# Windowed attention with a token-mixing layer on one core: a kernel planned in Python in place of one written batch by batch

## The chip, the core and the metric

The kernel runs on one core of a Trainium2 chip. Its time is the device time of one execution in microseconds; the median of several runs counts. The engines are TensorE (PE; its weight loads are PEld), VectorE (DVE), ScalarE (ACT), GpSimd (POOL) and SyncE (SP). Each takes its own instructions in the order in which they stand in the program and waits for semaphores of the others. Products of TensorE are written to PSUM, eight banks of 512 f32 per partition, from where VectorE and ScalarE copy them to SBUF.

## What is computed

Eight batches of 576 positions, 8 heads of 64. First attention with a window of 128 positions and a linear distance penalty, then a layer that mixes positions, on the attention's output x (576 x 512 per batch).

```python
# attention, per batch and head
scores = q @ k.T / 8 - 2.0**-(h+1) * |i - j|      # only where 0 <= i - j < 128
x[:, 64*h : 64*h+64] = softmax(scores) @ v
# mixing, per batch
mixed = ((x @ w_q) @ (x @ w_k).T / 8) @ x
out = relu(mixed) @ w_out
```

Inputs and output are f32 in DRAM; the kernel computes in f16 with f32 sums.

## The kernel before

**Tiling.** Positions go in tiles of 128, 128, 128, 128 and 64. The scores are kept transposed, keys on the partitions: for key tile kb the queries 128 kb to 128 kb + 255 are the only ones that the window lets through, so a head has five products of 256, 256, 256, 192 and 64 queries, 1024 columns in all, two PSUM banks.

**Loads** (`c_load`, L98 to L119). All on GpSimd's queue, with a cast from f32 to f16: per batch ten of q and k and five of v, each 128 (or 64) positions by 8 heads by 64. The tiles of q and k have one buffer each, so the loads of the next batch wait until TensorE has transposed this batch's.

**Attention.** `mk_xpose` (L121) transposes q and k, four heads' pairs at a time, and copies them out of PSUM. `mk_qk2` (L135) makes the scores of two heads into two PSUM tiles; ScalarE takes exp of 1024 columns (L152), VectorE multiplies by the table of exp(-slope * distance), zero outside the window (L153). `mk_pv` (L157) multiplies with V for one query tile and four heads (L179); V has a column of ones, so that the row sums come with it. VectorE divides (L182, L183). `mk_xt` (L189) transposes x.

**Mixing** (`moe_chunks`, L216). `wq` and `wk` project; the sum is regrouped as (x w_q) ((x w_k)^T x), so `gmat` (L248) makes a 64 x 512 matrix per batch; `mk_mixed` (L258) multiplies and takes relu; `mk_out` (L272) projects, copies to f32 and stores on SyncE's queue.

**Order.** Written by hand: the steps of attention of batch b stand in twelve chunks, and after each chunk one of mixing of batch b - 1. A framework moves instructions a little by their dependencies and gives each engine its list. All eight batches pass in this way, and the mixing of the last one stands alone at the end.

## Time and profile before

| | |
|---|---|
| time, median of 3 runs | 246.55 us (246.26 to 247.41) |
| span of the profiled execution | 246.7 us |
| TensorE busy | 211.7 us (86%), 1864 products |
| VectorE busy | 142.0 us (58%), 362 instructions |
| ScalarE busy | 121.5 us (49%), 218 instructions |
| GpSimd busy | 106.6 us (43%), 132 instructions |
| DMA from GpSimd's queue | 114096 packets, 14.82 MB |

Matmuls are pipelined, and a product's shown duration holds its way through the array; what a product costs in a row of them is the distance between the starts of two. The clock column is the one that the throttle granted to TensorE: 1.00 is 2.4 GHz, 0.50 is 1.2 GHz. At the start of the execution the column is 1.00 without a record of the clock, and there the distances of the starts have to be read instead.

### The profile page before, as it was taken

Reading aid. Unit: us, or ns where it says so; the run is one execution under the profiler, and the core shown is the slowest. Engines: PE = TensorE matmul, PEld = TensorE weight load, DVE = VectorE, ACT = ScalarE, POOL = GpSimd, SP = SyncE. Lnnn points to the kernel's source line nnn. Section 1 sums busy time; section 2 is a strip of 40 time slices with the busy share of each in tenths; the row PEclk is TensorE's granted clock in tenths of the full one; section 3 lists DMA queues with packets and bytes.
Section 4 is the critical chain, followed back from the end, with each engine's and each line's share of the span. In section 5 each row is a group of like instructions: output and inputs, shape, how many; then the busy total and the mean of one; then the engine's idle time right before and its main releaser. Section 6 shows DMA issues by size and latency. Waiting matters only on the chain.

```text
span 246.7 us, 4766 instructions
## 1 busy us (share of the span) xinstructions
PE 211.7 (86%) x1864; PEld 128.1 (52%) x1864; DVE 142.0 (58%) x362; ACT 121.5 (49%) x218; POOL 106.6 (43%) x132
## 2 busy tenths in 40 slices
PE   0367799889997999889997999889988999889783
PEld 0134576455564656456554656446554656556331
DVE  1124763567645775577556674667656774577413
ACT  2986505880179305970289106950389007930240
POOL 9999938900694019800792039700891000000000
PEclk9999999957996599857995599858995699759979
DMA  3999999972699039962999139922999131003204
GB/s 24 104 141 148 155 112 113 131 50 73 123 166 121 14 117 159 155 39 85 133 163 104 43 90 179 154 20 108 129 161 84 47 125 26 0 0 130 64 24 168
DMA packets 119366, 24.55 MB, mean 100 GB/s; under 512 B 114224, under 2 KB 114736, under 8 KB 119344
## 3 DMA queue, kind: packets, MB, share of 16 engines
q0 software_dynamic: 114096, 14.82, 93.3%
q1 hardware_dynamic: 5248, 9.44, 10.8%
q8 instruction: 14, 0.23, 0.4%
q14 instruction: 8, 0.07, 0.1%
HBM read 29.62 MB, written 9.44 MB: 158 GB/s over the span
## 4 chain that ended last, share of the span: by engine, by line
PE 65%; ACT 13%; DVE 7%; POOL 6%; issue 6%; DMA 2%; ACTq 0%; POOLq 0%
PE po L279 19%; PE px L179 15%; PE ptr L130 7%; PE pxt L198 5%; PE pw L226 4%; PE pk L240 3%; ACT rm L268 2%; DVE osb L51 2%; PE pm L266 2%; DMA vnat<-in_v_dram 2%; ACT qT L49 1%; POOL vnat L113 1%; ACT gm L49 1%; DVE invr L182 1%; PE pg L252 1%
## 5 line engine op out<-in xcount | busy, mean ns | idle before, releaser
L113 POOL DMA_DIRECT2D vnat<-in_v_dram x40 | 34.4, 885 | 77.5 <-issue 59.3
L49 ACT COPY qT<-ptr 128x512 f16<-128x512 f16 (+1 forms) x24 | 12.4, 517 | 80.8 <-PE ptr L130 80.8
L279 PE MATMUL po<-wout_sb,rm 128*128 128x512 f16 x160 | 50.4, 451 | 0.7 <-ACT rm L268 0.2
L143 PEld LDWEIGHTS <-kT 64*128 64x128 f16 x320 | 27.4, 106 | 25.5 <-issue 17.7
L51 DVE COPY osb<-po 128x512 f32<-128x512 f32 (+1 forms) x40 | 27.6, 690 | 19.6 <-PE po L279 19.2
L279 PEld LDWEIGHTS <-rm 128*128 128x128 f16 x160 | 17.1, 116 | 17.3 <-issue 10.1
L182 DVE RECIPROCAL invr<-px 128x4 f32<-128x4 f32 (+1 forms) x80 | 13.3, 175 | 19.8 <-PE px L179 18.3
L51 DVE COPY kT<-ptr 128x512 f16<-128x512 f16 (+1 forms) x24 | 9.1, 381 | 20.0 <-PE ptr L130 18.8
L268 ACT ACTIVATE rm<-pm 128x512 f16<-128x512 f32 x32 | 19.7, 631 | 0.5 <-PE pml L267 0.5
L266 PE MATMUL pm<-wqT,gm 64*128 64x512 f16 x32 | 14.1, 474 | 5.8 <-ACT gm L49 0.7
L51 DVE COPY xT<-pxt 128x512 f16<-128x512 f16 (+1 forms) x40 | 15.5, 388 | 1.0 <-PE pxt L198 0.5
L49 ACT CAST wqT<-pw 64x512 f16<-64x512 f32 x8 | 4.6, 579 | 16.8 <-PE pwl L228 16.8
L49 ACT COPY kT<-ptr 128x512 f16<-128x512 f16 x16 | 9.4, 586 | 5.8 <-PE ptr L130 5.8
L226 PE MATMUL pw<-xT,wqk_sb 128*64 128x512 f16 x32 | 10.1, 416 | 0.0
L51 DVE COPY qT<-ptr 128x512 f16<-128x512 f16 x16 | 6.7, 421 | 3.0 <-PE ptr L130 2.3
L269 ACT ACTIVATE rm<-pml 128x64 f16<-128x64 f32 x32 | 8.5, 264 | 0.0
L51 DVE CAST wkn<-pk 128x256 f16<-128x256 f32 (+1 forms) x16 | 4.4, 315 | 5.6 <-PE pk L240 5.6
L252 PEld LDWEIGHTS <-wkn 128*64 128x64 f16 (+1 forms) x40 | 3.7, 108 | 7.4 <-issue 3.3
L266 PEld LDWEIGHTS <-gm 64*128 64x128 f16 x32 | 3.0, 95 | 8.0 <-ACT gm L49 1.0
L240 PE MATMUL pk<-wqk_sb,xT 128*128 128x64 f16 (+1 forms) x160 | 7.1, 195 | 0.0
L267 PE MATMUL pml<-wqT,gm 64*128 64x64 f16 x32 | 6.7, 208 | 0.0
L240 PEld LDWEIGHTS <-xT 128*128 128x128 f16 (+1 forms) x160 | 5.8, 100 | 1.5 <-issue 0.2
(752 smaller groups left out, 562.0 us busy)
## 6 DMA issues: line engine op xcount, KB each, us to landing
out_dram<-osb SPq DMA_DIRECT2D x32, 256.0 KB, 2.0
vnat<-in_v_dram POOLq DMA_DIRECT2D x32, 128.0 KB, 5.0
out_dram<-osb SPq DMA_DIRECT2D x8, 128.0 KB, 4.0
vnat<-in_v_dram POOLq DMA_DIRECT2D x8, 64.0 KB, 4.7
wout_sb<-in_moe_w_out_dram POOLq DMA_DIRECT2D x1, 512.0 KB, 6.2
qnat_107<-in_q_dram POOLq DMA_DIRECT2D x1, 128.0 KB, 3.5
knat_109<-in_k_dram POOLq DMA_DIRECT2D x1, 128.0 KB, 3.4
qnat_111<-in_q_dram POOLq DMA_DIRECT2D x1, 128.0 KB, 3.4
```

What stands on the lines that cost most here:

```text
L49: eng.copy(out_ap, in_ap)
L51: eng.tensor_copy(out=out_ap, in_=in_ap)
L113: nc.gpsimd.dma_start(out=vnat[:n, kt, 0:H, 1:65], in_=v[b, :, ss, :].transpose([1, 0, 2]))
L130: nc.tensor.transpose(pt[:, c, :n], src, identh[:n, :n])
L143: nc.tensor.matmul(pss[i][:, o : o + w], kT[hb : hb + 64, hp, 128 * kb : 128 * kb + 128], qT[hb : hb + 64, hp, 128 * kb : 128 * kb + w], s ...
L179: nc.tensor.matmul(px[:, hh, :], lt, rt, start=(i == 0), stop=(i == len(mms) - 1))
L182: nc.vector.reciprocal(out=invr[:n], in_=px[:n, :, 0])
L226: nc.tensor.matmul(pw[0:64], wqk_sb[:, dc, 0:64], xT[:, dc, 0:512], start=(dc == 0), stop=(dc == 3))
L240: nc.tensor.matmul(pk[:n, t, :], xT[:, dc, 128 * t : 128 * t + n], wqk_sb[:, dc, 64:128], start=(dc == 0), stop=(dc == 3))
L266: nc.tensor.matmul(pm, lt, st_["wqT"][:, 0:512], start=True, stop=True)
L268: nc.scalar.activation(out=rm[:, db, 0:512], in_=pm, func=AF.Relu, scale=WSCALE)
L279: nc.tensor.matmul(po, rm[:, db, lo : lo + 128], wout_sb[:, db, :], start=(db == 0), stop=(db == 3))
```

## The change

The kernel is written anew. A small planner in Python (`Plan`) is given about 600 steps, each with the engines that may run it, an assumed duration for each, a priority, what it reads and writes, and how many PSUM banks it needs. It lays the steps out in assumed time, picks an engine for the copies that ScalarE or VectorE can make, assigns the banks (four double slots), and the program is emitted in that order; the framework keeps it.

- **Loads.** q, k and v of two batches come in one DMA of 128 x 16 x 64 (the first two batches' q and k in separate ones), into double buffers. The last 64 positions of two batches share one tile of 128. v of the first two batches, and the weights, come as f32 over SyncE's queue and are cast by ScalarE and VectorE.
- **Transposes.** Eight of 128 columns into one bank, copied out as 1024 columns at once.
- **Scores.** A unit is two heads and half of the key tiles: two banks, six or four products, in turn for the one head and the other, whose operands lie on partitions 0 to 63 and 64 to 127. One exp and one multiply of 1024 columns each as before, eight per batch.
- **Products with V.** 18 for two heads, over all five query tiles, always with 128 keys: the rows beyond the last key are zero in V, and the probabilities are padded. One reciprocal and one division for 2 x 5 x 64 columns, four of each a batch.
- **x transposed** two heads at a time, one copy of 576 columns.
- **Mixing.** The query projection is made twice over (128 columns of weights), in two halves of 288 queries; the Gram step in two halves of 256 columns that land on partitions 0 to 63 and 64 to 127; the mixed products in pairs on the two halves of the rows. The output of the last 64 positions is made for two batches in one tile, so there are 36 output tiles in place of 40.
- **Set-up.** The distance table is made of iota and VectorE's comparisons, 512 columns a head, and copied for the second form.

```diff
-        chunks = [[c_load, mk_xpose(0, 0), mk_xpose(1, 0), mk_xpose(0, 1), mk_xpose(1, 1)],
...
-    for b in range(NB):
-        ac, ast = attn_chunks(b)
...
+class Plan:
+    LAT = 0.10
...
+                    st = max(free.get(e, 0.0), t, tp)
+                    cand.append((st, o, e, dur))
+            assert cand, "the plan is stuck"
+            st0 = min(c[0] for c in cand)
+            near = [c for c in cand if c[0] <= st0 + 0.06]
+            st, o, e, dur = min(near, key=lambda c: (c[1].prio, c[1].seq, c[0] + c[3]))
+            for g in o.ps_new:
+                _, _, s, h = place(g, held)
+                g.slot = (s, h)
+                held[g.cls] = held.get(g.cls, 0) + g.banks
+                for i in range(g.banks):
+                    halves[s][h + i] = g
+            o.start, o.eng = st, e
+            free[e] = st + dur
...
+
+def act_t(n):
+    return 0.14 + 0.000833 * n
+
+
+def dve32_t(n):
+    return 0.13 + 0.00104 * n
+
+
+def dve16_t(n):
+    return 0.13 + 0.00052 * n
+
+
+PERIOD = 14.8
+NPT = 6
...
+    plan = Plan(4, {"score": 4, "other": 6})
...
+    def load(name, dst, src, n, prio, writes, merged=False):
+        plan.op(name, {"POOL": 0.47 + 0.00047 * n}, lambda e: nc.gpsimd.dma_start(out=dst, in_=src),
+                prio, writes=writes, lat=-0.00095 * n)
...
+                else:
+                    load("ldqk", nat[x][p % 2][:, j].rearrange("t b (h d) -> t (b h) d", h=H),
+                         src[2 * p : 2 * p + 2, :, tk, :].rearrange("b h t d -> t (b h) d"), 2048, t0,
+                         [("nat", x, p % 2, j, b) for b in range(2)])
...
+                    n = TN[t]
+                    load_f32("ldvf", osb[t][:n].rearrange("t (h d) -> t h d", h=H),
+                             v[b, :, 128 * t : 128 * t + n, :].transpose([1, 0, 2]), 8 * n, 64,
+                             t0 + 30 * b, [("osb", t)])
+                for t in range(NT):
+                    n = TN[t]
+                    cast("cv", vn[0][:n, t, b, :, 0:D], osb[t][:n].rearrange("t (h d) -> t h d", h=H), 512,
+                         -10 + 20 * b, [("osb", t)], [("vn", 0, t, b)])
...
+        for h in range(H):
+            def table(e, h=h):
+                nc.scalar.activation(out=bt[:, 1, h], in_=wm, func=AF.Exp, scale=-(2.0 ** (-(h + 1))))
+            plan.op("table", {"ACT": 0.6}, table, t0, reads=["wm"], writes=[("bt1", h)])
...
+                def tr(e, c=c, x=x, g=g):
+                    for hp in range(4):
+                        for j in range(2):
+                            o = hp * 256 + j * 128
+                            nc.tensor.transpose(ps16(g)[:, o : o + 128],
+                                                nat[x][pb][:, 2 * c + j, i, 128 * hp : 128 * hp + 128], idn)
+
+                def ev(e, c=c, x=x, g=g):
+                    cp(e, qkT[pb][:, i, x, :, 256 * c : 256 * c + 256],
+                       ps16(g).rearrange("t (a n) -> t a n", a=4))
+
+                plan.op("tqk", {"PE": 0.46}, tr, t0, ps_new=[g],
+                        reads=["idn"] + [("nat", x, pb, 2 * c + j, i) for j in range(2)])
+                plan.op("etqk", both(1024, True), ev, t0, ps_read=[g], writes=[("qkT", pb, i, x, c)])
...
+    CHUNK = [[(0, 0, 256), (1, 256, 256)], [(2, 0, 256), (3, 256, 192), (4, 448, 64)]]
...
+                def sc(e, hp=hp, c=c, g=g):
+                    for kb, o, w in CHUNK[c]:
+                        for a in range(2):
+                            r = slice(64 * a, 64 * a + 64)
+                            nc.tensor.matmul(ps32(g)[:, 512 * a + o : 512 * a + o + w],
+                                             qkT[pb][r, i, 1, hp, 128 * kb : 128 * kb + 128],
+                                             qkT[pb][r, i, 0, hp, 128 * kb : 128 * kb + w],
+                                             start=True, stop=True)
+
+                def ex(e, c=c, pt=pt, g=g):
+                    nc.scalar.activation(out=pt[:, c, 0:1024], in_=ps32(g), func=AF.Exp, scale=SCALE)
+
+                def mu(e, hp=hp, c=c, pt=pt):
+                    o = pt[:, c, 0:1024]
+                    nc.vector.tensor_tensor(
+                        out=o, in0=o, in1=bt[:, c, 2 * hp : 2 * hp + 2].rearrange("t h c -> t (h c)"),
+                        op=ALU.mult)
+
+                rd = [("qkT", pb, i, x, cc) for x in range(2) for cc in ((0, 1) if c == 0 else (1, 2))]
+                plan.op("sc", {"PE": 0.27}, sc, t0 + c * 1.5, ps_new=[g], reads=rd + ["pads"])
+                plan.op("exp", {"ACT": 0.95}, ex, t0 + c * 1.5, ps_read=[g], writes=[("pt", n, c)])
+                plan.op("mul", {"DVE": 0.68}, mu, t0 + c * 1.5,
+                        reads=["bt%d" % c and ("bt0", hp)], writes=[("pt", n, c)])
...
+            def pv(e, hp=hp, pt=pt, g=g):
+                for a in range(2):
+                    h = 2 * hp + a
+                    for t in range(NT):
+                        mm = []
+                        for kb, off in ((t - 1, 128), (t, 0)):
+                            if kb < 0:
+                                continue
+                            c = 0 if kb < 2 else 1
+                            o = 512 * a + (448 if kb == 4 else 256 * (kb % 2)) + off
+                            mm.append((pt[:, c, o : o + 128], vn[pb][:, kb, i, h, :]))
+                        for x, (lt, rt) in enumerate(mm):
+                            o = 512 * a + (D + 1) * t
+                            nc.tensor.matmul(ps32(g)[:, o : o + D + 1], lt, rt,
+                                             start=(x == 0), stop=(x == len(mm) - 1))
...
+            def nrm(e, hp=hp, iv=iv, g=g):
+                px = ps32(g).rearrange("t (a c) -> t a c", a=2)[:, :, 0 : NT * (D + 1)]
+                px = px.rearrange("t a (j e) -> t a j e", j=NT)
+                nc.vector.reciprocal(out=inv[iv], in_=px[:, :, :, D])
+                nc.vector.tensor_tensor(
+                    out=xs[i][:, :, 128 * hp : 128 * hp + 128].rearrange("t j (a d) -> t a j d", a=2),
+                    in0=px[:, :, :, 0:D],
+                    in1=inv[iv].unsqueeze(3).broadcast_to([P, 2, NT, D]),
+                    op=ALU.mult)
+
+            plan.op("pv", {"PE": 0.60}, pv, t1, ps_new=[g],
+                    reads=[("pt", n, 0), ("pt", n, 1)] + [("vn", pb, t, i) for t in range(NT)])
+            plan.op("nrm", {"DVE": 1.02}, nrm, t1, ps_read=[g], writes=[("xs", i, hp)])
...
+            def xt(e, hp=hp, g=g):
+                for t in range(NT):
+                    m = TN[t]
+                    nc.tensor.transpose(ps16(g)[:, lo[t] : lo[t] + m],
+                                        xs[i][:m, t, 128 * hp : 128 * hp + 128], idn[:m, :m])
+
+            def ext(e, hp=hp, g=g):
+                cp(e, xT[i][:, hp, 0:S], ps16(g)[:, 0:S])
+
+            plan.op("xt", {"PE": 0.30}, xt, t2, ps_new=[g], reads=[("xs", i, hp)])
+            plan.op("ext", both(S, True), ext, t2, ps_read=[g], writes=[("xT", i, hp)])
...
+        def mwq(e):
+            for c in range(2):
+                for dc in range(4):
+                    nc.tensor.matmul(ps32(g2)[:, 512 * c : 512 * c + 288], wqq[:, dc, :],
+                                     xT[i][:, dc, 288 * c : 288 * c + 288], start=(dc == 0), stop=(dc == 3))
...
+        def mg(e):
+            for t in range(NT):
+                m = TN[t]
+                for a in range(2):
+                    nc.tensor.matmul(ps32(g3)[64 * a : 64 * a + 64, 0:256], wkn[i][:m, t, :],
+                                     xs[i][:m, t, 256 * a : 256 * a + 256], start=(t == 0), stop=(t == NT - 1))
...
+                def mm(e, c=c, j=j, g=g4):
+                    for a in range(2):
+                        r = slice(64 * a, 64 * a + 64)
+                        nc.tensor.matmul(ps32(g)[:, 512 * a : 512 * a + 288], gm[i][r, 128 * j : 128 * j + 128],
+                                         wqT[i][r, 288 * c : 288 * c + 288], start=True, stop=True)
...
+            def mo(e, o=o, g=g5):
+                for db in range(4):
+                    nc.tensor.matmul(ps32(g), rm[pb][:, db, o : o + 128], wout[:, db, :],
+                                     start=(db == 0), stop=(db == 3))
+
+            def eo(e, n=n, g=g5):
+                cp(e, osb[n], ps32(g))
...
+            to = t0 + 6 + z * PERIOD / len(tiles)
+            rd = [("rm", pb, y, c, j) for y in ((i,) if t < 4 else (0, 1)) for c in range(2) for j in range(2)]
+            plan.op("po", {"PE": 0.90}, mo, to, ps_new=[g5], reads=rd + [("wout", c) for c in range(4)])
+            plan.op("eo", both(512), eo, to, ps_read=[g5], writes=[("osb", n)])
+            plan.op("st", {"SP": 0.2}, st, to, reads=[("osb", n)], lat=2.0)
...
+    order = plan.run()
+    with tc.manual_schedule():
+        for o in order:
+            o.emit(o.eng)
```

Where the order moved, at three places. ScalarE's list from the last exp of a batch to the first of the next, in the middle of the program. Before (`rm` is the relu of the mixing of the batch before, `qT` and `kT` the copies of the next batch's transposes, `ptr` their PSUM tile, `pw` that of the query projection):

```order
L152 ACTIVATE pt_1057<-ps_1_1043 128x1024
L268 ACTIVATE rm<-pm 128x512
L269 ACTIVATE rm<-pml 128x64
L54 ACTIVATE vnat<-identh 128x45
L54 ACTIVATE kT<-bfull_88 128x4x64
L49 COPY qT<-ptr 128x4x128
L49 COPY kT<-ptr 128x4x128
L49 CAST wqT<-pw 64x512
L49 CAST wqT<-pwl 64x64
...
L152 ACTIVATE pt_1399<-ps_0_1387 128x1024
```

After, from the last exps of the seventh batch into those of the eighth (`pt`; `psl` is any PSUM slot, `xT` the transposed x, `osb` an output tile of an earlier batch, `wkn`, `wqT` projections):

```order
L436 ACTIVATE pt_84<-psl_110 128x1024
L436 ACTIVATE pt_84<-psl_111 128x1024
L240 COPY xT_93<-psl_109 128x576
L240 COPY osb_106<-psl_110 128x512
L436 ACTIVATE pt_85<-psl_111 128x1024
L436 ACTIVATE pt_85<-psl_109 128x1024
L240 COPY xT_93<-psl_110 128x576
L436 ACTIVATE pt_86<-psl_111 128x1024
L240 COPY osb_103<-psl_110 128x512
L436 ACTIVATE pt_86<-psl_109 128x1024
L240 COPY osb_104<-psl_110 128x512
```

Before, the copies of a batch stand together between two blocks of exps; in the middle of the new list one to four exps stand side by side, and copies of this batch and of others stand between them.

ScalarE's list at the start, up to the first exp. Before (`bfull` are the tables, `wm` the distances):

```order
L64 ACT_TABLE_LOAD
L64 CAST identh<-ident_68 128x128
L49 COPY qT<-ptr 128x4x128
L84 ACTIVATE bfull_88<-wm 128x1024
...
L54 ACTIVATE kT<-bfull_88 128x4x64
L49 COPY kT<-ptr 128x4x128
L49 COPY qT<-ptr 128x4x128
...
L152 ACTIVATE pt_209<-ps_0_197 128x1024
```

After (`vn` is V, `osb` an output tile that holds V in f32 for the time being, `bt` the tables, `wkf` and `rm` hold weights in f32):

```order
L240 ACT_TABLE_LOAD
L240 CAST vn_77<-osb_107 64x8x64
L240 CAST vn_77<-osb_103 128x8x64
L240 CAST vn_77<-osb_104 128x8x64
L331 ACTIVATE bt<-wm 128x512 x8
L240 CAST wkw<-wkf 128x256
L240 COPY qkT_79<-psl_109 128x4x256
L240 CAST wout<-rm_102 128x512 x2
L436 ACTIVATE pt_81<-psl_110 128x1024
```

Three casts of V, which wait for loads on SyncE's queue, now stand ahead of the tables, and three casts of weights ahead of the first exp.

TensorE's list in the attention of a batch. Before (`po` is an output tile of the batch before, `px` the product with V of one query tile, `pt` the probabilities of one head, `x` the result that is transposed into `pxt`):

```order
L279 LDWEIGHTS rm
L279 MATMUL po<-wout_sb,rm 128x512
...
L179 LDWEIGHTS pt_1819
L179 MATMUL px<-vnat,pt_1819 128x65
...
L179 LDWEIGHTS pt_1822
L179 MATMUL px<-vnat,pt_1822 128x65
...
L198 LDWEIGHTS x_1929
L198 MATMUL pxt<-identh,x_1929 128x128
```

After (the rows of one pair of heads, of the next pair's scores, of an output tile and of the scores again):

```order
L465 LDWEIGHTS pt_84
L465 MATMUL psl_108<-vn_78,pt_84 128x65
L430 LDWEIGHTS qkT_80
L430 MATMUL psl_111<-qkT_80 128x256
...
L582 LDWEIGHTS rm_101
L582 MATMUL psl_110<-wout,rm_101 128x512
...
L430 LDWEIGHTS qkT_80
L430 MATMUL psl_109<-qkT_80 128x192
```

Before, products with V run over eight heads for one query tile, and the transposes of x follow tile by tile; now 18 products of one pair of heads stand together, and scores, output products and transposes of three batches alternate.

## Rows read from the trace of the kernel before

**Rows 1.** Windows: busy of PE, PEld, DVE, ACT, POOL; clock; DMA share; GB/s.

```profile
117.00:146.00 29.00, 26.98 (x248) 16.63 (x248) 18.29 (x49) 13.94 (x26) 12.58 (x16) 0.82 1.10 112
```

**Rows 2.** Longest wait: engine, line, releaser: us in total, times, longest.

```profile
ACT qT L49 <- PE ptr L130: 80.8, 8, 11.5
```

**Rows 3.** Chain of work that ended last: start us, us, engine, tile, line.

```profile
126.90 0.59 ACT pt_1822 L152
154.22 0.59 ACT pt_2242 L152
...
229.75 0.55 PE pw L226 x2
236.64 6.06 PE po L279 x20
```

**Rows 4.** Timeline of TensorE early: start us, us, engine, line, operation.

```profile
30.72 0.62 PE L198 MATMUL pxt<-identh,x_286 128*128 128x128 f16 x4
31.13 0.32 PE L179 MATMUL px<-vnat,pt_209 128*128 128x65 f16 x2
...
43.47 0.28 PE L143 MATMUL ps_1_548<-qT,kT 64*128 64x256 f16 x1
43.47 0.28 PE L143 MATMUL ps_0_547<-qT,kT 64*128 64x256 f16 x1
```

**Rows 5.** Timeline of TensorE, 59 to 64 us, at the higher clock.

```profile
59.46 0.22 PE L179 MATMUL px<-vnat,pt_559 128*128 128x65 f16 x2
...
59.95 0.39 PE L198 MATMUL pxt<-identh,x_709 128*128 128x128 f16 x4
60.41 1.02 PE L279 MATMUL po<-wout_sb,rm 128*128 128x512 f16 x4
61.27 0.33 PE L179 MATMUL px<-vnat,pt_559 128*128 128x65 f16 x2
...
63.41 0.40 PE L198 MATMUL pxt<-identh,x_748 128*128 128x128 f16 x4
```

**Rows 6.** Half a microsecond in which the clock falls (columns as above).

```profile
48.50:49.00 0.50, 0.50 (x6) 0.27 (x3) 0.44 (x1) 0.50 (x3) 0.50 (x2) 0.70 2.30 147
```

**Rows 7.** Timeline of ScalarE in the attention of a batch.

```profile
49.58 1.04 ACT L152 ACTIVATE pt_613<-ps_1_599 128x1024 f16<-128x1024 f32 x1
50.48 0.62 ACT L268 ACTIVATE rm<-pm 128x512 f16<-128x512 f32 x1
```

**Rows 8.** Groups by form: count | busy us, mean ns | idle before.

```profile
L49 ACT COPY kT<-ptr 128x512 f16<-128x512 f16 x16 | 9.4, 586 | 5.8 <-PE ptr L130 5.8
L51 DVE COPY osb<-po 128x512 f32<-128x512 f32 x32 | 22.1, 689 | 17.3 <-PE po L279 16.9
L51 DVE COPY kT<-ptr 128x512 f16<-128x512 f16 x16 | 6.8, 425 | 17.6 <-PE ptr L130 17.5
```

**Rows 9.** Timeline of VectorE in the attention of a batch.

```profile
52.06 0.18 DVE L182 RECIPROCAL invr<-px 128x4 f32<-128x4 f32 x1 [0.70 <-PE px L179]
52.27 0.42 DVE L183 TENSOR_TENSOR x_646<-px,invr 128x256 f16<-128x256 f32 x1
52.62 0.68 DVE L153 TENSOR_TENSOR pt_634<-pt_634,bfull_100 128x1024 f16<-128x1024 f16 x1
53.21 0.68 DVE L153 TENSOR_TENSOR pt_637<-pt_637,bfull_102 128x1024 f16<-128x1024 f16 x1
```

**Rows 10.** Timeline of the start: first load, first exp.

```profile
2.17 1.08 POOL L104 DMA_DIRECT2D qnat_107<-in_q_dram  x1
...
17.23 1.02 ACT L152 ACTIVATE pt_209<-ps_0_197 128x1024 f16<-128x1024 f32 x1 [0.70 <-PE ps_0_197 L143]
```

**Rows 11.** Timeline of GpSimd's loads of q and k for the second batch.

```profile
24.31 1.06 POOL L104 DMA_DIRECT2D qnat_432<-in_q_dram  x1
25.17 1.07 POOL L107 DMA_DIRECT2D knat_434<-in_k_dram  x1
```

**Rows 12.** DMA issues: tile, queue, count, KB, median us from issue to landing.

```profile
vnat<-in_v_dram POOLq DMA_DIRECT2D x32, 128.0 KB, 5.0
```

583 lines of the change are left out of this document (337 added, 246 removed).

## The prediction, made before the changed kernel was run

> **What bounds the kernel now.** Four views were read, in this order. The windows first: in 29 us of the steady part TensorE is busy for 26.98, VectorE for 18.29, ScalarE for 13.94 and GpSimd for 12.58, at a mean clock of 0.82 [rows 1]. So one engine is nearly always at work and the others stand idle by turns. The waits say what the turns are: the longest in total is ScalarE at the first copy of a batch's q transposes, 80.8 us in 8 times [rows 2]. Between two batches ScalarE has nothing to do, because TensorE first finishes the weighted sums and the output projection of one batch and only then transposes the next. The chain of waits shows the result, a fixed period: the same exp returns at 126.90 and 154.22, 27.3 us apart [rows 3]. Last comes TensorE's own timeline, for what it does in these 27.3 us. After about 59 us 16 products with V take 0.49 us (59.46 to 59.95), but for the last query tile, where 128-row and 64-row operands alternate, 16 take 2.14 us (61.27 to 63.41) [rows 5]: 1.65 us a batch, 13 in all.
>
> **What the change does to the busy time.** It is a new program, so I price its instructions from rows and add them up by engine, over all eight batches and without the set-up.
>
> ScalarE. The exps keep their form, and one follows the other instruction 0.90 us later (49.58 to 50.48), though it is shown with 1.04 us [rows 7]; so 0.14 us of an instruction lies under the next one when that is ready. 64 exps x 0.90 = 57.6. The wide f32 copies from PSUM: 0.62 us for 512 columns [rows 7], less 0.14, plus 64 columns at (1.04 - 0.62) / 512 us = 0.05: 0.53 for the 20 relus and 5 copies of 576, 13.3; 0.48 for 19 of 512, 9.1; 0.32 for 6 of 320 and 0.27 for 8 of 256, 4.1. The f16 copies: 0.586 us for 512 [rows 8], less 0.14, at the same slope: 0.86 for 19 of 1024 columns, 16.4; 0.50 for 15 of 576, 7.5. Sum 108 us. With the 0.14 left in for all 156, 130 us.
>
> VectorE. 64 multiplies at 0.59 (52.62 to 53.21) [rows 9]: 37.8. A reciprocal takes 0.21 to the next start, a normalising product of 256 columns 0.35 (52.27 to 52.62) [rows 9]; 384 more columns at (689 - 420) / 256 ns [rows 8, 9] are 0.40: 0.96 x 32 = 30.7. Copies, each less the 0.09 by which the multiplies overlap: 17 f32 of 512 at 0.60 [rows 8], 10.2; 15 of 576 at 0.67, 10.0; 17 f16 of 576 at 0.40, 6.8; 17 f16 of 1024 between 0.34 and twice that, I take 0.65, 11.0; two small ones 0.8. Sum 107 us, or 125 without overlap.
>
> TensorE at the higher clock. A 128-column transpose took 0.10 us early on (30.72 to 31.13 for four), at the lower clock [rows 4]; half of it, 0.051, for 416, and the 32 short ones: 22.1. Score products of two heads, which lie on different rows of the array, start at the same moment (both at 43.47) [rows 4], so 64 units cost the 512 columns of one head each, 0.215 at the pace of the output projection (0.86 us for four of 512, 60.41 to 61.27) [rows 5]: 13.8. Products with V, now all 128-row, 0.031 each [rows 5] x 576: 17.6; the 160 of the key projection at the same price: 5.0. Output projection 0.86 x 36: 31.0. The query projection, 64 of 288 columns at 0.121: 7.7. The 80 of the Gram step fall on two halves of the columns; nothing in the trace shows such a pair: side by side 4.3, one after the other 8.6, I take 4.3, since the row pairs do run together. The mixing, 32 row pairs at 0.121: 3.9. Sum 105 us, 110 at the other bound. The edge tiles now shared by two batches (36 output tiles for 40) and the padded last key tile are in these counts.
>
> So the change puts three engines at some 13.4 us a batch each, where now one of them rules 27.3.
>
> **The sum.** I follow ScalarE, which has the highest bound, through the span.
> First exp: now at 17.23, 15.1 us after the first load is issued [rows 10]. The eight loads that the first scores need are now issued one after another, 0.86 us apart (24.31 to 25.17) [rows 11], and land after 5.0 [rows 12]: about 2.2 + 7 x 0.86 + 5.0 = 13.2, then 16 transposes at 0.10, a copy and the scores, 16.0. Against this, ScalarE's order begins with three casts of V that wait for f32 loads on SyncE's queue; such a load is not in the trace. Landed by 8 us they cost nothing (three casts at 0.45 and eight tables at 0.48 then end near 13); if the 4608 rows of V and 1500 of weights take the DMA engines from q and k at the same 0.86 us per 1024, everything lands 5 us later and the first exp is near 22. I take **18.5**.
> Steady work: 108 us if everything follows closely, 130 if every instruction begins only when the one before it has ended, as it must where it waits for a result written just before. In the new order ScalarE changes every one to four instructions between exps and copies of fresh PSUM, so I take **124**. That holds the idle time of the three engines waiting for one another.
> The first batch: at 30.7 us the transposes still run at 0.10 us [rows 4], the lower clock, and the changed kernel's first batch has no mixing to fill TensorE. Its share of TensorE, about 7 us, doubles; half of it hides under exps: **5**, bounds 0 and 8.
> The end: after the last exp come a multiply (0.68), the sums (0.55), the normalising (1.0), transpose and copy (0.8) and handoffs, about 3.3 us; then the same serial row as now, projections, Gram step, mixing, five output tiles, from 229.75 to 246.7: 17.0 [rows 3], its 20 output products at 6.06 included. Of these 20.3 us ScalarE works 7.0, counted above: **13.5**.
> 18.5 + 124 + 5 + 13.5 = **161 us**. The profiled span is 246.7, the median 246.55; nothing is to be added.
>
> Loads: 101,000 rows still pass GpSimd at 0.86 us per 1024, 85 us, under 140; a pair's loads are issued two batches ahead, so I cost them at nothing. If the cover goes, rival 3.
>
> **A rule weighed.** The half microsecond in which the clock falls in the steady part (0.70 of the window, from 1.00 to half) shows TensorE busy 0.50 of 0.50 us [rows 6]. The Trainium skill ("TensorE: Matmul & The Clock Gate", "HAM oscillation — how this bites in real kernels") puts such falls down to gaps in which TensorE waits. The row disagrees: there was no such gap. By the page the changed kernel, with fewer gaps, would keep 2.4 GHz once it has it, and rival 1 would have no chance.
>
> **The rivals.**
> 1. The clock keeps falling as now. At a mean of 0.82 [rows 1] TensorE's 105 to 110 us become 128 to 134. Then TensorE is the path: 18.5, 131, 12 at the end (20.3 less 8.5 of its own work) and the same 16 us of waits for one another that the sum allows ScalarE (124 less 108): 178. For it: now it falls while TensorE is busy. Against: it falls just ahead of the exps of [rows 7], where score products of half the array's rows are nearly alone; the new order puts output products (512 columns, full height) between them all the time.
> 2. The pairs don't run together (the change doesn't do what it says): scores, Gram step and mixing take twice as long, 13.8 + 4.3 + 3.9 = 22 us more on TensorE, 127 to 132: by the sum of rival 1 about 177. Against: the score rows.
> 3. Loads late, or the fixed order too tight: TensorE's order has the second pair's transposes in the middle of the second batch, and an engine that waits there holds everything behind it. Each pair late by 8 us gives 161 + 24 = 185; up to 200.
> 4. Slower than before: TensorE at 1.2 GHz all along. 2 x 105 = 210, with 18.5, 12 and the 16 of waits: 257. It decides from a mean clock of about 0.53 (105 / 200); now it is 0.82 with less dense work.
> 5. Overlap as good as the 0.90 rows everywhere: 161 - 14 = 147.
>
> **How the numbers follow.** The forecast (150 to 172): 0.62. Rival 1: 0.15. Rival 2: 0.05. Rival 3: 0.10. Rival 4: 0.02. Rival 5: 0.06. Below the range 148 to 186 I leave 0.06, above it 0.10. A difference of 0.5% is about what can be told from none; faster by more than that 0.97, within it 0.01, slower 0.02.
>
> **What would show it.** Right: a period of about 15.5 us between the same exps, TensorE, VectorE and ScalarE each busy above 80% in the middle, the clock at 1.00 from the second batch on, the waits spread thinly over many lines, 20 us after the last exp. Wrong: the clock row at 5 in the middle (1); paired the two heads' score rows starting one after the other, 0.11 us apart (2); TensorE idle on a DMA of q or k (3); first exp after 22.

## The result, and the profile of the changed kernel

The changed kernel takes 189.01 us (median of 4 runs, 187.97 to 189.5), the kernel before 246.41 on the same chip: a ratio of 0.764, 95% interval [0.760, 0.769]. The forecast was 161 us with a range up to 186. The direction was right, the time is 28 us above the forecast and 3 above the range. The profiled execution has a span of 187.6 us. Of the experiments below, e1, e7 and e11 had two of four runs in a slower state: there the time given is the median of the other two, and of e11, profiled in a slower run, only the time is used.

Its page, the slices of the span (40 of 4.7 us each):

```profile
PE   0041175978968899797799978989999998989790
...
DVE  6924145678976698488487857896878878496210
ACT  2029066678776696595689768786979786894651
...
PEclk9999999999999999999999999999999999999997
DMA  6999999999999999999999999941014014303226
```

The clock stays at full speed, where before it had a mean of 0.82 [rows 1]. From slice 8 on TensorE is busy 6 to 9 tenths, not a steady 9. DMA is at 9 up to slice 25, some 115 us.

Windows, with the columns of [rows 1] (length, busy of PE, PEld, DVE, ACT, POOL, clock, DMA share, GB/s):

```profile
40.00:60.00 20.00, 15.51 (x254) 11.43 (x252) 16.40 (x31) 15.25 (x20) 15.23 (x16) 1.00 3.20 143
60.00:80.00 20.00, 17.00 (x232) 10.99 (x232) 14.44 (x25) 14.36 (x20) 9.44 (x11) 1.00 2.43 182
...
120.00:140.00 20.00, 18.48 (x247) 11.91 (x246) 15.44 (x28) 15.43 (x22) 0.00 (x0) 1.00 0.25 78
```

Three engines share the work now: 17.0, 14.4 and 14.4 of 20 us, where [rows 1] had 27.0, 18.3 and 13.9 of 29.

The start and the end, answering [rows 10] and [rows 3]. ScalarE's timeline:

```profile
13.05 1.66 ACT L240 CAST vn<-osb 64x512 f16<-64x512 f32 x3 [11.03 <-DMA osb<-in_v_dram]
14.62 4.26 ACT L331 ACTIVATE bt<-wm 128x512 f16<-128x512 f32 x8
...
23.70 1.01 ACT L240 COPY qkT<-psl 128x1024 f16<-128x1024 f16 x1 [4.53 <-PE psl L381]
...
26.72 1.02 ACT L436 ACTIVATE pt<-psl 128x1024 f16<-128x1024 f32 x1 [0.97 <-PE psl L430]
...
43.19 1.95 ACT L436 ACTIVATE pt<-psl 128x1024 f16<-128x1024 f32 x2
...
154.25 1.95 ACT L436 ACTIVATE pt<-psl 128x1024 f16<-128x1024 f32 x2
...
166.73 1.94 ACT L436 ACTIVATE pt<-psl 128x1024 f16<-128x1024 f32 x2
```

The first exp (ScalarE's exponential of 1024 columns, eight a batch) starts at 26.72 (forecast 18.5), the ninth, with which the second batch begins, at 43.19, the 57th (the eighth batch) at 154.25: 111.06 us for six batches, a period of 18.5 us (forecast 15.5). The last exp ends at 168.7; 18.9 us follow (forecast 20.3). So the profiled 26.6 us above the forecast are 8.2 in the start, 19.8 between the first and the last exp (142.0 for 122.2) and -1.4 at the end. The start and the middle are two separate questions.

**The start** is answered by the chain of waits (start, us, what) and the DMA issues (as [rows 12]):

```profile
5.87 0.82 POOL natk L249
6.69 16.00 DMA natq<-in_q_dram
...
22.98 9.54 DMA natq<-in_q_dram
```

```profile
natq<-in_q_dram POOLq DMA_DIRECT2D x12, 256.0 KB, 14.2
...
osb<-in_v_dram SPq DMA_DIRECT2D x8, 256.0 KB, 8.2
```

The seventh of the eight loads that the first scores need is issued at 6.69 and landed 16.0 us later, where [rows 12] had 5.0. SyncE's queue (start, us to issue) brings V and the weights in the same stretch:

```profile
0.74 5.60 SPq L278 DMA_DIRECT2D osb<-in_v_dram  x5
...
8.88 0.89 SPq L278 DMA_DIRECT2D rm<-in_moe_w_out_dram  x1
```

ScalarE's wait of 11.03 us for that V, at 13.05 above, is not what delays the first exp: its next copy, at 23.70, waits for transposes.

**The middle** is answered by no row of the page: the chain goes through many short pieces of all engines. The timeline shows the pattern (start, us, engine, line, tiles, and in brackets the idle time before and what ended it):

```profile
57.10 0.59 PE L582 MATMUL psl<-wout,rm 128*128 128x512 f16 x2
...
57.53 0.52 PE L492 MATMUL psl<-idn,x 128*128 128x128 f16 x5
...
57.98 0.62 PE L381 MATMUL psl<-idn,natk 128*128 128x128 f16 x8
58.09 0.69 DVE L242 COPY osb<-psl 128x512 f32<-128x512 f32 x1 [0.46 <-PE psl L492]
...
58.54 0.39 PE L430 MATMUL psl<-qkT 64*128 64x256 f16 x6
...
58.81 0.64 ACT L240 COPY xT<-psl 128x576 f16<-128x576 f16 x1 [1.71 <-DVE osb L242]
58.86 0.72 PE L465 MATMUL psl<-vn,pt 128*128 128x65 f16 x18
...
59.35 1.02 ACT L240 COPY qkT<-psl 128x1024 f16<-128x1024 f16 x1
...
60.42 0.38 PE L582 MATMUL psl<-wout,rm 128*128 128x512 f16 x1 [0.84 <-ACT qkT L240]
```

Look for waits that the data don't explain. At 58.09 VectorE copies an output tile (osb), whose products ended at 57.69, but it waits for the transposes of x (57.53 to 58.05). ScalarE copies these transposes only at 58.81, when VectorE's copy of the output tile has ended (58.78): two reads of different data, one after the other. At 60.42 TensorE starts an output product when ScalarE's copy of q and k transposes has ended (60.37). In the planner's placement each of these pairs lies in the two halves of the same PSUM tile: the kernel declares four tiles of two banks (`psl`, 1024 columns) and gives their halves to units of one bank as if they were independent. With each start in the trace set against the data and the bank that the unit really needs by the plan, some 60 waits over 0.25 us are left over between the seventh and the last exp, about 35 us in all (how many depends a little on when a product is taken to have ended); nine in ten or more end with work on the other half of the same tile. The kernel before had two score tiles and four small ones, each for one unit at a time.

### The profile page after: what moved, and what is told of

Read it like the earlier page. It is cut to its first block, busy times and chain, and to the rows that moved or that the text cites. A ratio compares the mean times of both kernels' runs of the same rounds, so it can differ in the third digit from the quotient of the medians.

```text
span 187.6 us, 4468 instructions
## 1 busy us (share of the span) xinstructions
PE 140.8 (75%) x1856; PEld 92.4 (49%) x1856; DVE 124.3 (66%) x232; ACT 126.9 (68%) x172; POOL 69.7 (37%) x76
## 3 DMA queue, kind: packets, MB, share of 16 engines
q0 software_dynamic: 102512, 12.98, 132.4%
## 4 chain that ended last, share of the span: by engine, by line
PE 54%; DMA 14%; ACT 13%; DVE 10%; issue 4%; POOL 3%; ACTq 0%; DVEq 0%; POOLq 0%
PE psl L582 17%; DMA natq<-in_q_dram 14%; PE psl L465 7%; PE psl L381 7%; PE psl L492 7%; PE psl L430 5%; ACT qkT L240 5%; PE psl L525 4%; PE psl L539 3%; DVE xT L242 3%; ACT pt L436 3%; DVE osb L242 3%; PE psl L513 2%; ACT osb L240 2%; ACT xT L240 2%
## 5 line engine op out<-in xcount | busy, mean ns | idle before, releaser
L436 ACT ACTIVATE pt<-psl 128x1024 f16<-128x1024 f32 x64 | 63.8, 1034 | 4.4 <-PE psl L430 4.3
L440 DVE TENSOR_TENSOR pt<-pt,bt 128x1024 f16<-128x1024 f16 x64 | 42.7, 683 | 1.7 <-ACT pt L436 1.7
L582 PE MATMUL psl<-wout,rm 128*128 128x512 f16 x144 | 36.4, 380 | 3.4 <-ACT osb L240 0.9
L430 PE MATMUL psl<-qkT 64*128 64x256 f16 (+2 forms) x320 | 25.5, 265 | 2.1 <-ACT qkT L240 0.6
L475 DVE TENSOR_TENSOR x<-psl,inv 128x640 f16<-128x640 f32 x32 | 26.4, 825 | 1.1
L240 ACT COPY qkT<-psl 128x1024 f16<-128x1024 f16 x19 | 19.1, 1015 | 10.6 <-PE psl L381 6.3
L465 PE MATMUL psl<-vn,pt 128*128 128x65 f16 x576 | 24.1, 197 | 2.1 <-DVE pt L440 0.6
L249 POOL DMA_DIRECT2D natk<-in_k_dram x20 | 21.6, 1078 | 10.6 <-DMA natk<-in_k_dram 5.3
L249 POOL DMA_DIRECT2D natq<-in_q_dram x20 | 21.3, 1064 | 9.5 <-DMA natq<-in_q_dram 4.3
L465 PEld LDWEIGHTS <-pt 128*128 128x128 f16 x576 | 21.4, 99 | 6.7 <-issue 2.6
L242 DVE COPY qkT<-psl 128x1024 f16<-128x1024 f16 x17 | 11.6, 689 | 14.2 <-PE psl L381 11.7
L492 PE MATMUL psl<-idn,x 128*128 128x128 f16 (+1 forms) x160 | 16.8, 217 | 3.0 <-ACT qkT L240 1.8
L492 PEld LDWEIGHTS <-x 128*128 128x128 f16 (+1 forms) x160 | 11.5, 97 | 12.3 <-DVE x L475 3.1
## 6 DMA issues: line engine op xcount, KB each, us to landing
natq<-in_q_dram POOLq DMA_DIRECT2D x12, 256.0 KB, 14.2
```

The lines of the kernel that those rows point to most:

```text
L240: nc.scalar.copy(o, i)
L242: nc.vector.tensor_copy(out=o, in_=i)
L249: plan.op(name, {"POOL": 0.47 + 0.00047 * n}, lambda e: nc.gpsimd.dma_start(out=dst, in_=src), prio, writes=writes, lat=-0.00095 * n)
L430: nc.tensor.matmul(ps32(g)[:, 512 * a + o : 512 * a + o + w], qkT[pb][r, i, 1, hp, 128 * kb : 128 * kb + 128], qkT[pb][r, i, 0, hp, 128 * ...
L436: nc.scalar.activation(out=pt[:, c, 0:1024], in_=ps32(g), func=AF.Exp, scale=SCALE)
L440: nc.vector.tensor_tensor(out=o, in0=o, in1=bt[:, c, 2 * hp : 2 * hp + 2].rearrange("t h c -> t (h c)"), op=ALU.mult)
```

## The experiments

Exps are given by their start in the profiled run; a period is a sixth of the way from the ninth to the 57th. All ratios are to the kernel before on the same chip, where it took 246.4 to 247.3 us; e1 to e4, e5 to e8, e9 to e12 and e13 to e15 ran on four different chips, so differences of 1 us or less between these groups tell nothing.

| kernel | us | ratio, 95% | first exp | last exp | period |
|---|---|---|---|---|---|
| changed | 189.0 | 0.764 [0.760, 0.769] | 26.7 | 167.6 | 18.5 |
| e1 two tiles of four banks | 279.0 | 1.130 [1.116, 1.143] | 25.3 | 249.4 | 30.4 |
| e2 tiles split | 174.1 | 0.703 [0.698, 0.708] | 26.1 | 153.9 | 16.7 |
| e3 V by GpSimd | 183.2 | 0.743 [0.737, 0.749] | 17.3 | 159.8 | 17.7 |
| e4 no loads | 188.6 | 0.764 [0.759, 0.768] | 24.4 | 167.6 | 18.7 |
| e5 split, TensorE -23 | 172.0 | 0.697 [0.693, 0.702] | 25.8 | 152.7 | 16.5 |
| e6 split, ScalarE -27 | 173.5 | 0.702 [0.698, 0.706] | 28.1 | 152.8 | 16.6 |
| e7 split, V by batch | 169.0 | 0.684 [0.679, 0.690] | 14.6 | 149.2 | 17.6 |
| e8 split, true prices | 173.4 | 0.702 [0.698, 0.706] | 24.6 | 153.8 | 16.8 |
| e9 split, no loads | 172.5 | 0.700 [0.696, 0.704] | 25.3 | 153.5 | 16.4 |
| e10 split, VectorE -17 | 173.5 | 0.705 [0.700, 0.709] | 25.4 | 153.0 | 16.5 |
| e11 split, all three | 168.7 | 0.683 [0.678, 0.688] | | | |
| e12 all three, no loads | 156.0 | 0.631 [0.628, 0.634] | 27.8 | 136.7 | 14.2 |
| e13 no loads, TensorE -23 | 166.0 | 0.673 [0.667, 0.678] | 26.1 | 146.3 | 15.4 |
| e14 no loads, ScalarE -27 | 169.9 | 0.688 [0.684, 0.693] | 28.0 | 150.0 | 16.0 |
| e15 no loads, VectorE -17 | 171.4 | 0.693 [0.688, 0.698] | 25.4 | 151.7 | 16.1 |

"Split" is e2's arrangement of the tiles, "-23" the us of work taken from an engine, "no loads" without the loads of batches 2 to 7. Kernels with half an exp fill the whole probability tiles at the start, which brings their first exp near 28; the ninth is not later for it (e6 40.5, e2 40.5).

The theories, as the expectations name them. A: units that share a PSUM tile wait for one another. B: the loads of the first pair get in each other's way. C: the loads in the middle hold TensorE. D, E and G: TensorE, ScalarE or VectorE sets the pace by its work. F: none does, three engines with nearly the same work hold each other in a fixed order.

**Shared tiles, doubled (e1).** Same order, same banks; only the declaration differs:

```diff
-    psl = [pps.tile([P, 1024], FP32, name=f"psl{i}") for i in range(4)]
+    psl = [pps.tile([P, 2048], FP32, name=f"psl{i}") for i in range(2)]
...
+        h += 2 * (s % 2)
-        return psl[s][:, 512 * h : 512 * (h + g.banks)]
+        return psl[s // 2][:, 512 * h : 512 * (h + g.banks)]
```

> Same order of work and same banks; the PSUM is declared as two tiles of four banks instead of four tiles of two. Theory A (units that share a PSUM tile wait for one another, though they lie in different banks): after 36 us the changed kernel shows 67 waits of 0.25 us or more, 39 us in all, that end when work on the other half of the same tile ends; with three neighbours in place of one there are more of them: 205 to 230 us, the last exp from 167.6 to 183 or later. Theory B (the loads of the first pair) and theory C (the loads in the middle keep TensorE waiting): no change, 188 to 190.

Measured 279.0 us, slower even than the kernel before, far past the 230 expected. Counted as above there are some 200 such waits, about 200 us in all (several engines wait at once). The bytes lie where they lay, so neither the banks nor the data make the wait, but what the program declares as one tile. The clock fell too, which the expectation left out; how much of the missed 49 us is the clock's is not shown:

```profile
40.00:100.00 60.00, 40.83 (x464) 28.84 (x465) 29.57 (x51) 28.90 (x37) 33.35 (x33) 0.78 2.48 135
100.00:160.00 60.00, 43.54 (x458) 27.44 (x453) 27.68 (x48) 29.68 (x36) 8.68 (x10) 0.78 1.03 88
```

The Trainium skill ("PSUM — Partial Sum Buffer", "PSUM bank collisions raise a hardware error") tells of engines that must be kept apart in one bank and says that different banks run clean. The units here are in different banks, so by that page the chip asked for none of these waits.

**Shared tiles, removed (e2).** Three tiles of two banks for the units of two, two of one bank for the units of one:

```diff
+SIZES = [2, 2, 2, 1, 1]
-    psl = [pps.tile([P, 1024], FP32, name=f"psl{i}") for i in range(4)]
+    psl = [pps.tile([P, 512 * n], FP32, name=f"psl{i}") for i, n in enumerate(SIZES)]
...
-                    if halves[s] == [None, None]:
+                    if SIZES[s] == 2 and halves[s] == [None, None]:
...
-                else:
-                    for h in range(2):
-                        if halves[s][h] is None:
-                            c = (when[s][h], 0 if halves[s][1 - h] is not None else 1, s, h)
-                            best = c if best is None or c < best else best
+                elif SIZES[s] == 1 and halves[s][0] is None:
+                    c = (when[s][0], 0, s, 0)
+                    best = c if best is None or c < best else best
```

> Three PSUM tiles of two banks for the two-bank units, two tiles of one bank for the one-bank units, and the planner knows it, so that no two units ever share a tile; all else as in the changed kernel. Theory A: the waits for the other half of a tile are gone; from first to last exp 141 us becomes 121 to 128, the time 168 to 176. Theories B and C: 187 to 191, first to last exp 138 to 143.

174.1 us, 15 less, from first to last exp 127.8 for 140.9. Of the waits over 0.25 us that neither data nor bank explains at most two are left. In the stretch shown above each copy now waits for its own products (output tile, transposes of x):

```profile
57.13 0.81 PE L581 MATMUL psl<-wout,rm 128*128 128x512 f16 x3
57.97 0.59 ACT L239 COPY osb<-psl 128x512 f32<-128x512 f32 x1 [0.16 <-PE psl L581]
58.19 0.53 PE L491 MATMUL psl<-idn,x 128*128 128x128 f16 x5
...
58.83 0.46 DVE L241 COPY xT<-psl 128x576 f16<-128x576 f16 x1 [1.39 <-PE psl L491]
```

Theory A holds: without shared tiles 13 of the 19.8 us in the middle are gone. The planner, given other slots, also made a new order, in which about a third of the steps stand elsewhere. In its own assumed time the two orders are equally long from first to last exp (119.1 and 119.6 us), so the order alone was not expected to gain, but no run separates it; e1, in the old order, shows that the declaration alone makes the waits.

**The loads at the start (e3).** The branch of `load_v` for the first pair is deleted, so its V takes the way of the others:

```diff
-        if p == 0:
-
-            for b in range(2):
-                for t in range(NT):
-                    n = TN[t]
-                    load_f32("ldvf", osb[t][:n].rearrange("t (h d) -> t h d", h=H),
...
-            return
```

> The first pair's V comes through GpSimd as that of the other pairs does, behind the first q and k, so the ten f32 loads on SyncE's queue and the ten casts are gone; the weights stay there. Theory B: the first q and k no longer share the DMA engines with V, the first exp comes at 18 to 21 instead of 26.7 and the time is 181 to 184; if the V rows, now behind q and k of the pair, hold the first products with V, a part is given back. Theories A and C: the first exp may move, but 187 to 191 in the end.

183.2 us (181.3 to 184.3); the first exp at 17.27, even earlier than expected. The chain:

```profile
3.22 6.98 DMA natq<-in_q_dram
...
17.41 9.64 DMA vn<-in_v_dram
27.09 2.69 PE psl L452 x46
```

The load of q on the chain, here the third, takes 7.0 us, and the seventh, issued at 6.72, lands after 6.9 where it took 16.0. But 9.5 us at the first exp are 3.6 at the ninth (39.60): the first products with V now wait for V, loaded for both batches at once. Theory B holds for the start. The Trainium skill ("DMA: Bandwidth & Descriptors", "Issuing engines are not separate DMA queues") says that transfers of all issuing engines run on the same 16 DMA engines and interleave; the 16.0 and 7.0 us agree.

**The loads in the middle (e4).** Batches 2 to 7 read the first pair's data:

```diff
-        plan.op(name, {"POOL": 0.47 + 0.00047 * n}, lambda e: nc.gpsimd.dma_start(out=dst, in_=src),
+        plan.op(name, {"POOL": 0.47 + 0.00047 * n}, lambda e: None if skip else nc.gpsimd.dma_start(out=dst, in_=src),
...
-                                                nat[x][pb][:, 2 * c + j, i, 128 * hp : 128 * hp + 128], idn)
+                                                nat[x][0][:, 2 * c + j, i, 128 * hp : 128 * hp + 128], idn)
```

> Batches 2 to 7 read q, k and V of batches 0 and 1 from where these lie, and their loads are left out; order of the compute work unchanged (the output is that of the first pair, four times). Theory C: TensorE no longer waits for q and k between 55 and 113 us; first to last exp 141 us becomes 128 to 133, the time 176 to 181. Theories A and B: 186 to 190, first to last exp 139 to 141.

188.6 us. The first exp comes 2.3 us earlier, but the 17th at 62.85 (changed kernel: 62.83), the 33rd at 99.95 (99.95), the last at 167.63 (167.64). The window from 60 us is the same to the digit, without a load:

```profile
40.00:60.00 20.00, 16.12 (x239) 12.09 (x236) 15.17 (x28) 14.14 (x19) 0.00 (x0) 0.91 0.02 7
60.00:80.00 20.00, 17.00 (x232) 10.99 (x232) 14.44 (x25) 14.36 (x20) 0.00 (x0) 1.00 0.13 49
```

That the two runs meet so exactly is luck: of the 2.3 us 1.1 are lost by the ninth exp (41.97), and the other 1.2 go where the granted clock is 0.50, from 43 to 46 us (the first line), which the changed kernel doesn't have. From 47 us on ScalarE's steps start within 0.05 us of each other with the loads and without. Theory C falls: DMA engines at 9 tenths for 115 us cost the middle of this kernel nothing.

**Which engine sets the pace of the split kernel (e5, e6, e8).** One product of four in the output projection; half an exp; the planner with the prices of the trace:

```diff
-                for db in range(4):
+                for db in range(1):
```

> Built on the kernel with three tiles of two banks and two of one bank (174.1 us, first exp 26.05, last 153.87). The output projection makes only the first of its four accumulated products, so the output is a part of the reference's; order and all other work unchanged. That takes 0.65 us x 36 = 23 us from TensorE, 20 of it before the last exp, and nothing from the others. Theory D (TensorE sets the pace between first and last exp, since its work was priced too low): first to last exp 127.8 us becomes 107 to 114, time 150 to 157. Theory E (ScalarE sets it, as forecast) or F (no engine: the handoffs of a fixed order): first to last exp 122 to 128, time 166 to 172, the end part 3 us shorter.

```diff
-                    nc.scalar.activation(out=pt[:, c, 0:1024], in_=ps32(g), func=AF.Exp, scale=SCALE)
+                    nc.scalar.activation(out=pt[:, c, 0:512], in_=ps32(g)[:, 0:512], func=AF.Exp, scale=SCALE)
```

> Built on the same kernel. Each exp covers 512 of its 1024 columns (the other half of each probability tile stays at one, so the output is not the reference's); order and all other work unchanged. That takes 64 x 0.43 = 27 us from ScalarE, nothing from the others. Theory E (ScalarE sets the pace, as forecast): first to last exp 127.8 us becomes 101 to 110, time 147 to 156. Theory D (TensorE): 124 to 128, time 170 to 174. Theory F (handoffs): something between, since each exp's result comes 0.43 us earlier: 115 to 124.

```diff
-    LAT = 0.10
+    LAT = 0.15
...
-                plan.op("sc", {"PE": 0.27}, sc, t0 + c * 1.5, ps_new=[g], reads=rd + ["pads"])
+                plan.op("sc", {"PE": 0.33}, sc, t0 + c * 1.5, ps_new=[g], reads=rd + ["pads"])
```

> Built on the same kernel: the planner orders with prices as the trace shows them (scores 0.33 for 0.27 us, products with V 0.64 for 0.60, Gram step 0.79 for 0.60, key projection 0.62 for 0.90, and so on, handoff 0.15 for 0.10). Theory F (the order is too tight because its prices were wrong): first to last exp 127.8 us becomes 120 to 124, time 166 to 170. Theories D and E: 126 to 129, time 172 to 176.

172.0, 173.5 and 173.4 us against 174.1: the most is 2 us, 1.4 of them after the last exp, and the ratios' intervals of all three overlap that of e2. D and E fall. F allowed for e5, and nearly for e6 (124.7 us from first to last exp, where it had up to 124), but of e8 it expected 120 to 124 us, and 129.1 came; so it seems to fall too, which leaves VectorE, the loads, or a case that the expectations had left out: two equal limits.

**VectorE, loads, and all at once (e9 to e12).** e9 has the edit of e4, e10 half a multiply (below), e11 the edits of e5, e6 and e10, e12 all four:

```diff
-                    o = pt[:, c, 0:1024]
+                    o = pt[:, c, 0:512]
```

> The kernel with three tiles of two banks and two of one bank, and batches 2 to 7 read q, k and V of batches 0 and 1 from where these lie; their loads are left out (the output is that of the first pair, four times). In the changed kernel itself the same edit gave nothing after the first batch. Theory C again (with the tiles split, TensorE runs into the loads, row by row): first to last exp 127.8 us becomes 116 to 122, time 160 to 168. Theories D, E, F, G (compute or order): 126 to 129, time 171 to 174 (the first exp 2 us earlier, as it was there).

> The split kernel; each multiply by the bias table covers 512 of its 1024 columns (so half of the products have no bias and the output is not the reference's), order unchanged. Takes 64 x 0.27 = 17 us from VectorE, nothing from the others. Theory G (VectorE sets the pace): first to last exp 127.8 becomes 112 to 117, time 158 to 164. Theory F (the fixed order and the handoffs between three engines that have nearly the same work): 123 to 128, time 170 to 174.

> The split kernel with all three reliefs at once: one product of four in the output projection, half an exp, half a multiply; order unchanged, output not the reference's. Takes 23 us from TensorE, 27 from ScalarE, 17 from VectorE. Theory F (each engine waits for the other two in turn, so that a relief of one alone gives nothing): now the whole pace falls by about the smallest relief, first to last exp 104 to 114, time 150 to 160. Theory C (loads): it stays above 120, time 166 to 172.

> As the kernel with all three reliefs, and without the loads of batches 2 to 7. Theory C (the loads hold the relieved kernel): 15 us or more below the kernel with the three reliefs and its loads. Theory F: within 4 us of it.

The loads alone out: 172.5. VectorE alone relieved: 173.5. All three engines relieved: 168.7. The three relieved and the loads out: 156.0, 12.7 us below that, where theory C had expected 15 or more and F at most 4. A part goes through the clock: the share granted was 0.95 and 0.97 in the two runs of e11 that count and 0.99 in e12, by an estimate (0.04 of 167 us less 0.01 of 154) 5 us at the most. The rest fits two limits of nearly the same length in the split kernel, compute and loads, each of which alone hides what relief of the other gives back. The chain of e2 ran through the loads for a while:

```profile
83.89 1.14 POOL natq L248
85.03 1.15 POOL natk L248
86.17 1.10 POOL natq L248
87.28 16.09 DMA natk<-in_k_dram
103.84 11.54 DMA ntl<-in_k_dram
```

**One engine at a time without the loads (e13 to e15).** The edits of e5, e6 and e10, each with that of e4.

> The split kernel without the loads of batches 2 to 7 (172.5 us, exps 25.33 to 153.46) and with one output product of four; order unchanged, output not the reference's. 23 us less work for TensorE. Theory D (TensorE sets the compute pace, its pieces cost 125 us and not 105): first to last exp 128.1 becomes 110 to 116, time 156 to 161. Theories E, G (another engine) or F (all three hold each other): 123 to 128, 167 to 172.

> The same without the loads and with half an exp (27 us less for ScalarE) and whole output products. Theory E (ScalarE, as forecast): first to last exp 104 to 112, time 150 to 157. Theories D, G or F: 122 to 128, 167 to 172.

> The same without the loads and with half a multiply (17 us less for VectorE), the rest whole. Theory G (VectorE): first to last exp 112 to 116, time 157 to 161. Theories D, E or F: 123 to 128, 167 to 172.

Against 172.5: TensorE -6.6, ScalarE -2.7, VectorE -1.1 (the intervals of that last one overlap), together -10.4; all three at once -16.5. None falls towards 156 alone. TensorE weighs most: 166.0 lies between the range of theory D (156 to 161) and that of the others (167 to 172), so neither came out as written. What is left is a form of F in which the three hold each other in the fixed order and TensorE has the largest part. This is argued, not shown: no run changed the order alone or the number of PSUM slots with these reliefs in. Whether another order would do better stays open; that with the trace's prices (e8) was not faster.

**A faster version (e7).** The split tiles, V of the first pair one batch at a time behind that batch's q and k, and the weights held back behind a small write by GpSimd:

```diff
+                    load("ldv", vn[0][:n, t, b, :, 0:D],
+                         v[b, :, 128 * t : 128 * t + n, :].transpose([1, 0, 2]), 8 * n,
+                         (V0, V1)[b], [("vn", 0, t, b)])
...
+        plan.op("hold", {"POOL": 0.15}, lambda e: (nc.gpsimd.memset(wqf[:, 0, 0:1], 0.0), nc.gpsimd.memset(wof[:, 0, 0:1], 0.0)),
+                HOLD, writes=["wqf"] + [("rm", 1, i, c, j) for i in range(2) for c in range(2) for j in range(2)])
```

> Built on the same kernel: V of the first pair comes through GpSimd, one batch at a time (batch 0 behind q and k of batch 0, batch 1 behind q and k of batch 1), and the weights wait for a small write that GpSimd makes behind all these loads. Theory B (the f32 loads take the DMA engines from q and k): first exp at 16.5 to 18.5 instead of 26.05, and since V no longer comes ahead of the second batch's q and k, most of the 8 us stays: 164 to 168 us. Against it: what q and k gain V of the first batch loses, the ninth exp stays at 40 and the time at 172 to 175.

169.0 us, some 10% under the changed kernel, between the two ranges expected. The first exp is at 14.58, 11.5 us earlier than in e2, yet the last only 4.7: the 17th, the first of the second pair, is at 54.62 for 58.45, since that pair's loads now come last on GpSimd. The chain of waits up to 63.6 us is GpSimd's issuing and two loads, so there the loads are the limit; from 58 to 75 us the clock is at 0.80 besides.

## Why the prediction was wrong, by its steps

**First exp, 18.5 with bounds 16 to 22: too low by 8.2.** The cause was named (V and weights take the DMA engines from q and k), its size was not: I let everything land 5 us later. The load on the path took 16.0 us instead of 5.0, since eight other transfers were issued on SyncE's queue in the first 9 us, the last of them of 1 MB. With V behind q and k instead the seventh load lands after 6.9 us and the first exp is at 17.3 (e3), inside the bounds.

**ScalarE's 124 us of steady work and 5 for the first batch: too low by 19.8.** Two steps failed.
The first is one that the sum doesn't have. The 16 us for "the idle time of the three engines waiting for one another" meant waits for data. The waits for the other half of a PSUM tile, 13 us (e2, with its new order), were in none of the terms and none of the rivals, though the diff shows the declaration: four tiles of 1024 columns and half-tile slots in the planner.
The second is the choice of ScalarE as the path. The prices of ScalarE and VectorE came out as worked out (an exp 0.91 us after the one before, a copy of 1024 columns 0.91, a normalising 0.99). TensorE's did not. From the start of a group of products to that of the next, in the lower quarter of the cases, 64 score units take 0.33 us each, 36 groups of eight transposes 0.46, 32 groups of five 0.34, 32 with V 0.64, eight Gram steps 0.79, and the rest as forecast: 123 us, not 105. I priced the columns and put at nothing the change between products of a different shape (128 rows or 64, 128 columns of weights or 64). The trace has 171 such changes, and the product after one starts at least 0.094 us later than the columns before it ask for, in the lower quarter 0.098: 16.7 of the 18 us. A change of group at the same shape costs 2 ns in the lower quarter of 84. In the rows above six score products of 64 rows start at 58.54 and products of 128 rows at 58.86: 0.32, where 512 columns are 0.215. The price stood in [rows 5], in the very place that the prediction reads first: 16 products that alternate between 128 and 64 rows take 1.65 us more than 16 of one height, 0.10 each. So three engines have 108, 107 and 123 us, none of them far ahead, and a period of 16.4 without loads and shared tiles (e9) for the forecast 15.5: 0.9 x 7 batches is about the other 6 us. That these 6 us come of the three engines' nearly equal work is argued from e13 to e15, not shown.

**The end, 20.3: right,** 18.9. **The loads at nothing:** right for the middle (e4), wrong for the start, and no longer true once the tiles are split (e9, e12).

**The rivals.** 1, a falling clock: no, 1.00 in every window of the middle. The rule of the Trainium skill that the prediction weighed ("TensorE: Matmul & The Clock Gate", "HAM oscillation — how this bites in real kernels") said so, and it came out: with fewer gaps the clock stayed. e1 puts gaps back in and has 0.78. What the single row of before [rows 6] shows against it stays unexplained. 2: no. The two heads' score products start 2 to 33 ns apart, half of the 160 pairs within 5 (100.654 and 100.657 for one), and the pairs of the Gram step 3 to 30, 37 of the 40 within 4; in turn they would be 107 apart, by an estimate of 256 columns at the pace of [rows 5]. That the Gram step takes 0.79 us, where 0.54 would be side by side and 1.07 in turn, is mostly two of the changes above: its last pair has 64 rows. 3, loads late or the order too tight: the time was near its 185, for its first reason only at the start, and for its second hardly (e8). 4 and 5: no.

The range ended at 186 because its top was rival 3 alone; late loads and a second mechanism together were not in it.

## What to carry to other kernels

Before pricing a plan, list which units share a declared buffer: a wait is made per tile as the program declares it, and shows in the trace as an engine that waits for an operation whose data it doesn't touch. When relief of one engine gives nothing, relieve it again with the next suspect out as well: two equal limits can hide each other, and busy shares near 90% on one of three balanced engines don't name the bound. Count how often TensorE goes between products of 128 and of 64 rows or columns of weights: 171 changes cost 16.7 us of its work here; whether an order that groups them would be faster was not tried. And price transfers that run before the first result by all that is issued in the same stretch, whichever queue it is on.

## What the runs showed of the hardware

The loads of 256-byte rows, halved to 128 bytes on the way, run at a plateau of 156 to 158 GB/s as the page counts it (the slices from 33 to 52 us), with 126 bytes a packet (12.98 MB in 102512). By an estimate that is 157 / 126 or 1.25 rows per ns for all DMA engines, 0.82 us per 1024, close to the 0.86 from issue to issue in [rows 11]; which of the two sets that pace is not shown. The two lines of the page of the changed kernel:

```profile
GB/s 123 177 157 282 158 158 157 156 158 156 156 140 104 181 219 190 158 138 235 203 158 184 222 189 129 81 169 59 0 62 166 3 28 141 115 0 133 96 47 232
...
q0 software_dynamic: 102512, 12.98, 132.4%
```

A change between products of 128 and of 64 rows, or columns of weights, costs TensorE some 0.1 us, also from one pair to the next within the Gram step, and a change of group without it 2 or 3 ns. Scores (64 rows) take 0.22 us before mixing products (64 rows), against the 0.32 above before products of 128 rows; eight transposes (128 rows) take 0.46 us before products with V (128 rows), against 0.56 above (57.98 to 58.54) before scores:

```profile
164.54 0.40 PE L430 MATMUL psl<-qkT 64*128 64x256 f16 x6 [0.37 <-DVE xT L242]
164.76 0.30 PE L555 MATMUL psl<-wqT,gm 64*128 64x288 f16 x2
...
132.48 0.62 PE L381 MATMUL psl<-idn,natk 128*128 128x128 f16 x8
132.94 0.71 PE L465 MATMUL psl<-vn,pt 128*128 128x65 f16 x18
```

The split kernel has 163 such changes and the kernel before 276; none of them costs less than 0.094 us.

And TensorE's busy share says little of a bound. In the split kernel (e2) it stands at 16.47 of 17 us and VectorE's at 13.40:

```profile
58.00:75.00 17.00, 16.47 (x232) 10.29 (x229) 13.40 (x24) 15.15 (x21) 6.98 (x9) 1.00 2.70 173
```

Yet 23 us less work on TensorE gave 2 us while the loads ran (e5), and 7 without them (e13).
